# Attention into a SoLU feed-forward on one core: q and k requested a quad ahead, the w_out product later, fewer additions, and a new order for the first quad

## The chip, the cores and the metric

The kernel runs on one core of a Trainium2 chip. The metric is device time in microseconds. Before the change three runs took 1051.24 to 1053.21 us, with a median of 1052.91.

## The reference

Attention with normalised q and k over 8 batches of 12 heads, 448 tokens, 64 wide, and behind it a feed-forward with a SoLU and a layer norm on the 3584 x 768 result. All in float32, while the three feed-forward weights arrive as float64.

```
q_n = q / sqrt(mean(q*q) + 1e-6) * g_q          # k likewise with g_k
attn = softmax(q_n @ k_n.T / 8)                 # per head, 448 x 448
x = (attn @ v), heads side by side              # 3584 x 768
h = x @ w_in                                    # 3584 x 1024
solu = h * softmax(h)
ln = (solu - mean) / sqrt(var + 1e-6) * g_ln
out = ln @ w_out                                # 3584 x 768
```

## The kernel before

Two heads of a batch form a pair (48 pairs), two pairs a quad (24 quads, `m`); within a quad the pairs are called a = 2m and b = 2m + 1. A quad is worked through in one hand-written order, line 930 on, in which each engine takes its instructions strictly as they are written:

- `load` (L543) asks for q and k of a pair: eight slices of 56 KB, each made of runs of 32 floats, on SyncE's queue. `load_v` (L558, L559) asks for v of the next quad, `load_w` (L458) for one chunk of a weight.
- `squares` (ScalarE, L564), `row_sums` (VectorE, L569), `swap_sums` and `fold_sums` (GpSimd, L582, L586) give the sums of squares; `rsqrt_seed` (ScalarE, L593 to L595) and `rsqrt_step` (GpSimd, L600 to L603) the reciprocal root; `normalise` (GpSimd, L608) the normalised q and k, through one buffer; `qk_transpose` (VectorE, L618) turns them, and `gain` (ScalarE, L622) scales q. Only then can `scores` of that pair start.
- `scores` (TensorE, L636) puts 128 keys against 448 queries for two heads, three times per pair; `scores_last` (L648) does the last 64 keys of both pairs at once. Each is followed by an exponential on ScalarE (L629) into a tile E. Two PSUM tiles serve the scores in turn.
- `values` and `values_last` (TensorE, L686, L675) multiply with v. `sums` (TensorE, L711) forms the softmax sums by a product with ones; `add` (L662, L665) adds E tiles up beforehand, so that fewer products are needed. `inverse` and `divide` (VectorE, L719 to L736, GpSimd, L725) finish x.

While the first quads run, the weights are converted from float64 by bits, chunk by chunk: `low_bits` (ScalarE, L473, L474), `high_bits` (VectorE, L477, L478), `join` (VectorE, L482), and for w_out a `product` with g_ln (ScalarE, L487). The twelve chunks of w_in go with pairs 0 to 11 (`W_IN = 12`), the sixteen of w_out, one or two per pair, with pairs 12 to 21 (`W_OUT = 22`). `begin(n)` starts the chunks of a pair, `step(n)` takes them one of the four steps on, `end(n)` takes them on and then asks for as many new chunks; three raw buffers hold what has arrived.

From quad 6 on, two pieces of feed-forward run in each quad (`ff`: the hidden product L754 in two halves; the maximum L764, exponential L767 and the rest of SoLU follow on VectorE and ScalarE), from quad 11 on up to eight, with the output product (L809) among them. In quads 6 to 9 one half hidden product stands behind `scores_last` and one behind `sums`; quad 10 has the latter alone.

In `add`, pairs before 12 add E0 and E1 on VectorE and leave the rest to two more terms of `sums`; pairs from 12 on add E0 and E1 on GpSimd and two more tiles on VectorE, and `sums` has one term.

Of the kernel before, what the change touches and what calls it, by code (L numbers as in the profile page):

```python
# [14 lines left out]
OP = AluOpType  # L15
# [351 lines left out]
def fast_path(  # L367
# [286 lines left out]

    def add(n, kc):
        d = st[n]
        if kc == 1:
            d["es"] = work.tile([P, 2, S], FP32, tag="es", name="es")  # L660
            e = nc.vector if n < W_IN else nc.gpsimd
            e.tensor_tensor(d["es"], d["E", 0], d["E", 1], OP.add)  # L662
        elif n >= W_IN:
            pp, x = (slice(0, P), d["E", kc]) if kc < NJ else (slice(n % 2 * D, n % 2 * D + D), quads[n // 2]["E", NJ])
            nc.vector.tensor_tensor(d["es"][pp], d["es"][pp], x[pp], OP.add)  # L665

    def values_last(m):

# [22 lines left out]
    def sums(m):  # L691

        d = quads[m]
        early = 2 * m < W_IN
        if early:
            sm = ps_h.tile([P, DFF], FP32, tag="h", name="sm")[:, 0:S]
        else:
            sm = ps_t.tile([P, S], FP32, tag="t", name="sm")
        d["sm"] = sm
        terms = [lambda i: (ones[:, 0], st[2 * m + i]["es"])]  # L700
        if early:
# [146 lines left out]
    def load_next():  # L848
        if len(raws) < len(wq):
            raws.append(load_w(wq[len(raws)]))  # L850
# [13 lines left out]
    def step(n):  # L864
        for c in sets[n]:
            c.pop(0)()

    def end(n):

        step(n)  # L870
        for _ in sets[n]:
            load_next()
        step(n)


    events = []
# [21 lines left out]
    def prepare(n):  # L898
        squares(n)
        row_sums(n)  # L900
        swap_sums(n)
        fold_sums(n)
# [2 lines left out]
    load(1)  # L905
    load_gains()
    setup()
    for _ in range(2):
        load_next()
    load(2)  # L910
    load_next()
    load(3)
    load_v(0)
    with tc.manual_schedule():
        prepare(0)
        squares(1)
        rsqrt_seed(0)
        rsqrt_step(0)
        normalise(0)
        row_sums(1)  # L920
        swap_sums(1)
        fold_sums(1)
        gains()
        qk_transpose(0)
        gain(0)
        rsqrt_seed(1)
        rsqrt_step(1)
        normalise(1)
        at = 0
        for m in range(NQ):  # L930
            a, b = 2 * m, 2 * m + 1
            due = []

            while at < len(events) and len(due) < (8 if a >= W_OUT else 2) and events[at][0] <= a:
                due.append(events[at][1])
                at += 1

            def ff(k):
                for f in due[len(due) * k // 4 : len(due) * (k + 1) // 4]:
                    unit(f)  # L940

            more = m + 1 < NQ
            ring = "o"
            unit(lambda: scores(a, 0))
            if m == 0:
                qk_transpose(1)
            else:
                step(a)
            unit(lambda: scores(a, 1))
            gain(b)  # L950
            if m == 0:
                begin(0)
                prepare(2)
            if a >= W_IN:
                add(a, 1)
            ff(0)
            unit(lambda: scores(a, 2))
            unit(lambda: scores_last(m))
            if a < W_IN:
                add(a, 1)  # L960
            if m == 0:
                begin(1)
                prepare(3)
            else:
                end(a)
                if a >= W_IN:
                    begin(b)
            if a >= W_IN:
                add(a, 2)
            ff(1)  # L970
            unit(lambda: scores(b, 0))
            unit(lambda: scores(b, 1))
            if a >= W_IN:
                add(b, 1)
                add(a, 3)
            elif m == 0:
                step(0)
                end(0)
            ff(2)
            unit(lambda: scores(b, 2))  # L980
            if a < W_IN:
                add(b, 1)
            else:
                add(b, 3)
                add(b, 2)
# [7 lines left out]
            def outputs():  # L993
                values_last(m)
                values(a)
# [8 lines left out]
            if more:  # L1004
                qk_transpose(a + 2)
                begin(a + 2)
                normalise(b + 2)
            if m + 2 < NQ:
                swap_sums(a + 4)
                fold_sums(a + 4)  # L1010
            unit(lambda: values(b))
            if m + 2 < NQ:
                load(b + 4)
                squares(b + 4)
                row_sums(b + 4)
            if more:
                gain(a + 2)
                if b + 2 < W_IN:
                    begin(b + 2)
                qk_transpose(b + 2)  # L1020
            if m + 2 < NQ:
# [5 lines left out]
            if more:  # L1027
# [25 lines left out]
def kernel(  # L1053
# [30 lines left out]

    def bound_scores():

        nc.vector.tensor_tensor(gg[:, 0], gg[:, 0], gg[:, 1], OP.mult)
        nc.vector.tensor_reduce(gmax, gg[:, 0], AX, OP.max, apply_absolute_value=True)
        nc.vector.tensor_scalar(large, gmax[0:1], 80.0 / float(D) ** 0.5, None, OP.is_gt)
        nc.vector.tensor_scalar(within, gmax, 80.0 / float(D) ** 0.5, float(D) ** -0.5, OP.is_le, OP.mult)  # L1090
# [36 lines left out]
```

## Time and profile before

| what | value |
|---|---|
| time, median of 3 runs | 1052.91 us |
| profiled execution | 1053.97 us, span 1052.2 us |
| TensorE busy, mean granted clock | 965.3 us (92%), 0.966 |
| VectorE, ScalarE, GpSimd busy | 536.9, 362.4, 318.4 us |
| DMA | 70.09 MB, mean 67 GB/s |

The program is one stream of quads. Early in the span TensorE has gaps, and its records are longer where the granted clock is low; from about 300 us on it is full. A matmul of this kernel shows as two records, so the four matmuls of one `sums` term are eight records.

### The profile page before, as it was taken

What the parts mean: (1) busy time and instruction counts of PE and PEld (TensorE: products, weight loads), DVE (VectorE), ACT (ScalarE), POOL (GpSimd) and SP (SyncE); (2) the same over time, 40 slices, a digit from 0 to 9 for tenths busy, and PEclk for the clock granted to TensorE, in tenths of its full rate; (3) what the DMA queues carried; (4) which work ended last, traced back from release to release, by engine and by line L of the source; (5) the groups of instructions that cost most, each with busy time, mean ns of one, the idle gap of its engine ahead of it and who ended that gap; (6) DMA issues with size and microseconds to landing.
All of it is one profiled execution on the core that took longest, in us unless ns stands there. A gap on an engine that the chain in (4) does not pass through costs nothing.

```text
span 1052.2 us, 10821 instructions
## 1 busy us (share of the span) xinstructions
PE 965.3 (92%) x3619; PEld 428.6 (41%) x3619; DVE 536.9 (51%) x771; ACT 362.4 (34%) x621; POOL 318.4 (30%) x642
## 2 busy tenths in 40 slices
PE   3797887788699999999999999999999999999997
PEld 1232222233134444444444444444444443455554
DVE  3576767667764353534344454434453643555431
ACT  4566754445532232232233232322323323111110
POOL 2455463455344141413141322324141403100000
PEclk9799998898699999999999999999999999999999
DMA  7555544243321121203030302121120001434410
GB/s 150 130 127 115 121 83 97 66 98 77 71 54 44 40 53 30 49 20 67 16 68 16 67 25 45 37 46 43 40 59 24 18 16 33 155 114 123 132 61 34
DMA packets 235961, 70.09 MB, mean 67 GB/s; under 512 B 225136, under 2 KB 225144, under 8 KB 235896
## 3 DMA queue, kind: packets, MB, share of 16 engines
q1 hardware_dynamic: 228152, 57.84, 25.3%
q10 hardware_dynamic: 7744, 11.47, 2.9%
q8 instruction: 30, 0.49, 0.2%
q14 instruction: 35, 0.29, 0.1%
HBM read 58.27 MB, written 11.01 MB: 66 GB/s over the span
## 4 chain that ended last, share of the span: by engine, by line
PE 74%; DVE 6%; ACT 5%; SPq 5%; POOL 4%; DMA 3%; issue 2%; ACTq 0%; POOLq 0%; DVEq 0%
PE po L809 27%; PE h L754 25%; PE s L636 10%; PE o L686 6%; SPq L543 4%; PE s L648 2%; PE pu L798 2%; ACT E L629 2%; DMA v<-in_v_dram 2%; POOL qkn L608 1%; PE sm L711 1%; PE o L675 1%; ACT sq L564 1%; POOL es L662 1%; DVE qkT L618 1%
## 5 line engine op out<-in xcount | busy, mean ns | idle before, releaser
L809 PE MATMUL po<-w_out,uT 128*128 128x384 f32 x896 | 298.6, 489 | 6.7 <-DVE r L719 3.4
L754 PE MATMUL h<-w_in,xT 128*128 128x512 f32 x672 | 302.2, 599 | 0.0
L809 PEld LDWEIGHTS po<-w_out,uT 128*128 128x128 f32 x896 | 167.9, 190 | 137.6 <-issue 16.7
L636 PE MATMUL s<-qkT 64*128 64x448 f32 x576 | 155.2, 646 | 60.3 <-ACT qkT L622 36.4
L754 PEld LDWEIGHTS h<-w_in,xT 128*128 128x128 f32 x672 | 124.9, 191 | 160.6 <-issue 152.3
L629 ACT ACTIVATE E<-s 128x896 f32<-128x896 f32 x168 | 149.6, 915 | 93.8 <-PE s L636 87.7
L665 DVE TENSOR_TENSOR es<-es,E 128x896 f32<-128x896 f32 (+1 forms) x72 | 78.4, 1089 | 96.0 <-ACT E L629 65.3
L662 POOL TENSOR_TENSOR es<-E 128x896 f32<-128x896 f32 x36 | 76.3, 2118 | 158.4 <-ACT E L629 158.3
L782 POOL TENSOR_TENSOR he<-he,mhalf 128x1 f32<-128x1 f32 x28 | 17.5, 624 | 329.9 <-DVE he L781 329.9
L686 PE MATMUL o<-E,v 128*64 128x448 f32 x576 | 114.0, 545 | 0.0
L636 PEld LDWEIGHTS s<-qkT 64*128 64x128 f32 x576 | 52.0, 205 | 150.8 <-ACT E L629 49.8
L810 ACT COPY y<-po 128x384 f32<-128x384 f32 x56 | 26.8, 479 | 219.6 <-PE po L809 219.6
L800 DVE COPY uT<-pu 128x512 f32<-128x512 f32 x28 | 19.3, 688 | 160.1 <-PE pu L798 92.2
L767 ACT ACTIVATE u<-h,hmax 128x1024 f32<-128x1024 f32 x28 | 31.2, 1114 | 157.0 <-DVE hmax L764 157.0
L569 DVE TENSOR_REDUCE part<-sq 128x28 f32<-128x896 f32 x48 | 51.6, 1074 | 65.6 <-ACT sq L564 65.6
L608 POOL TENSOR_TENSOR qkn<-qk,ny 128x896 f32<-128x896 f32 x47 | 79.7, 1696 | 15.1 <-DMA qk<-in_k_dram 4.0
L764 DVE TENSOR_REDUCE hmax<-h 128x1 f32<-128x1024 f32 x28 | 34.0, 1215 | 82.1 <-PE h L754 82.1
L618 DVE STREAM_TRANSPOSE qkT<-qkn 128x896 f32<-128x896 f32 x48 | 53.1, 1106 | 34.6 <-POOL qkn L608 34.6
L686 PEld LDWEIGHTS o<-E,v 128*64 128x64 f32 x576 | 39.3, 138 | 74.4 <-issue 72.7
L564 ACT ACTIVATE sq<-qk 128x896 f32<-128x896 f32 x48 | 45.5, 949 | 67.7 <-DMA v<-in_v_dram 31.4
L582 POOL COPY ss<-part 32x28 f32<-32x28 f32 x188 | 40.1, 213 | 45.7 <-DVE part L569 26.7
L600 POOL TENSOR_TENSOR nx<-nx,ny 128x28 f32<-128x28 f32 x47 | 24.5, 521 | 89.1 <-ACT ny L595 89.1
(83 smaller groups left out, 705.7 us busy)
## 6 DMA issues: line engine op xcount, KB each, us to landing
qk<-in_q_dram SPq DMA_DIRECT2D x192, 56.0 KB, 2.6
out_dram<-y ACTq DMA_DIRECT2D x28, 384.0 KB, 2.3
qk<-in_k_dram SPq DMA_DIRECT2D x184, 56.0 KB, 2.2
v<-in_v_dram SPq DMA_DIRECT2D x96, 96.0 KB, 2.3
raw<-in_moe_w_in_dram SPq DMA_DIRECT2D x12, 512.0 KB, 4.3
raw<-in_moe_w_out_dram SPq DMA_DIRECT2D x16, 384.0 KB, 3.3
again<-in_moe_w_in_dram SPq DMA_DIRECT2D x13, 448.0 KB, 4.1
again<-in_moe_w_out_dram SPq DMA_DIRECT2D x13, 448.0 KB, 3.4
```

Of the source, the lines that this page charges most:

```text
L543: (nc.scalar if n < 2 and s else nc.sync).dma_start(d["qk"][g * 32 : g * 32 + 32, s], src[b, h0 + g // 2].rearrange("(b t) (x d) -> x t b ...
L564: nc.scalar.activation(d["sq"], d["qk"].rearrange("p s b d -> p (s b) d"), AF.Square)
L569: nc.vector.tensor_reduce(d["part"], d["sq"], AX, OP.add)
L608: first(n).tensor_tensor(d["qkn"], d["qk"].rearrange("p s b d -> p (s b) d"), d["y"].rearrange("p b -> p b ()").to_broadcast([P, 2 * NB, 32]),
L618: nc.vector.transpose(d["qkT"].rearrange("p s t -> p (s t)"), d["qkn"].rearrange("p b d -> p (b d)"))
L629: nc.scalar.activation(d["E", kc], s[:, :, 0:S], AF.Exp)
L636: nc.tensor.matmul(s[:, h, 0:S], d["qkT"][hh, 1, kc * P : (kc + 1) * P], d["qkT"][hh, 0, :], start=True, stop=True)
L662: e.tensor_tensor(d["es"], d["E", 0], d["E", 1], OP.add)
L665: nc.vector.tensor_tensor(d["es"][pp], d["es"][pp], x[pp], OP.add)
L686: nc.tensor.matmul(d["o"][h * D : (h + 1) * D, :], d["v"][:, h, kc], d["E", kc][:, h], start=False, stop=(kc == NJ - 1),)
L754: nc.tensor.matmul(d["h"][:, hs], xTs[m][:, c, i * P : (i + 1) * P], w_in[:, c, hs], start=(c == 0), stop=(c == KD - 1))
L809: nc.tensor.matmul(po, d["uT"][:, c], w_out[:, c, hs], start=(c == 0), stop=(c == KF - 1))
```

## The change

Loads: q and k of pairs a+4 and b+4 are requested together behind the second scores of pair a, no longer each just ahead of its squares. Before the loop the order is chunk, pair 2, pair 3, chunk, v, chunk.

`add`: pairs 12 to 21 now also add E0 and E1 on VectorE and leave the rest to `sums`, whose two more terms last until pair 21; the sums of quads 6 to 10 still use the same PSUM tile as before. From pair 22 on nothing is different.

Weights: the last step of a chunk, the product of w_out, leaves `end` and comes behind the second scores of pair b for pair a, and behind the values of pair b for pair b; the `begin` that follows moves with it.

First quad: pair 0's and pair 1's preparation are interleaved otherwise, the preparation of pairs 2 and 3 moves behind the last scores of pair a and the second of pair b, and the conversions of chunks 0 and 1 move behind the exponentials. Three small instructions on the gains go from VectorE to GpSimd.

```diff
-    def add(n, kc):
+    DVE, POOL = nc.vector, nc.gpsimd
+
+    def add(n, kc, engine):
         d = st[n]
+        busy = n < W_OUT
         if kc == 1:
-            d["es"] = work.tile([P, 2, S], FP32, tag="es", name="es")
-            e = nc.vector if n < W_IN else nc.gpsimd
-            e.tensor_tensor(d["es"], d["E", 0], d["E", 1], OP.add)
-        elif n >= W_IN:
+            if engine is (DVE if busy else POOL):
+                d["es"] = work.tile([P, 2, S], FP32, tag="es", name="es")
+                engine.tensor_tensor(d["es"], d["E", 0], d["E", 1], OP.add)
+        elif not busy:
...
     def sums(m):
...
-        if early:
+        if 2 * m < W_OUT:
             terms = [
...
     def end(n):
         step(n)
         for _ in sets[n]:
             load_next()
-        step(n)
...
     with tc.manual_schedule():
-        prepare(0)
+        squares(0)
+        row_sums(0)
+        swap_sums(0)
+        fold_sums(0)
         squares(1)
+        row_sums(1)
         rsqrt_seed(0)
         rsqrt_step(0)
+        gains()
         normalise(0)
-        row_sums(1)
...
             gain(b)
-            if m == 0:
-                begin(0)
-                prepare(2)
-            if a >= W_IN:
-                add(a, 1)
+            if next2:
+                load(a + 4)
+                load(b + 4)
+            add(a, 1, POOL)
             ff(0)
             unit(lambda: scores(a, 2))
             unit(lambda: scores_last(m))
...
             unit(lambda: scores(b, 1))
-            if a >= W_IN:
-                add(b, 1)
-                add(a, 3)
-            elif m == 0:
-                step(0)
-                end(0)
+            if m:
+                step(a)
+                if a >= W_IN:
+                    begin(b)
+            else:
+                prepare(3)
...
             unit(outputs)
-            if m + 2 < NQ:
-                load(a + 4)
+            if next2:
                 squares(a + 4)
                 row_sums(a + 4)
             end(b)
-            if more:
+            if next1:
                 qk_transpose(a + 2)
-                begin(a + 2)
+                if a < W_IN:
+                    begin(a + 2)
                 normalise(b + 2)
...
+            step(b)
+            if next1:
+                if a >= W_IN:
+                    begin(a + 2)
                 if b + 2 < W_IN:
                     begin(b + 2)
```

SyncE's queue before, from the last v of quad 0's end to the first of quad 1's; buffer numbers tell pairs apart: qk_502 and qk_537 are pairs 6 and 7, raw is a chunk.

```order
L558 DMA v_402<-in_v_dram 128x3x64 x2
L559 DMA vl_397<-in_v_dram 64x2x64
L458 DMA raw_449<-in_moe_w_in_dram 128x1024
L543 DMA qk_502<-in_q_dram 32x14x32 x4
L543 DMA qk_502<-in_k_dram 32x14x32 x4
L458 DMA raw_516<-in_moe_w_in_dram 128x1024
L543 DMA qk_537<-in_q_dram 32x14x32 x4
L543 DMA qk_537<-in_k_dram 32x14x32 x4
L558 DMA v_576<-in_v_dram 128x3x64 x2
```

The same place after the change; qk_434 and qk_443 are pairs 6 and 7.

```order
L558 DMA v_402<-in_v_dram 128x3x64 x2
L559 DMA vl_397<-in_v_dram 64x2x64
L543 DMA qk_434<-in_q_dram 32x14x32 x4
L543 DMA qk_434<-in_k_dram 32x14x32 x4
L543 DMA qk_443<-in_q_dram 32x14x32 x4
L543 DMA qk_443<-in_k_dram 32x14x32 x4
L458 DMA raw_467<-in_moe_w_in_dram 128x1024
L458 DMA raw_525<-in_moe_w_in_dram 128x1024
L558 DMA v_576<-in_v_dram 128x3x64 x2
```

The sixteen slices moved ahead of both chunks, and v stays last.

ScalarE before, in quad 6, from the gain of pair b to the last exponential; L629 are the exponentials, L487 the product of pair a's w_out chunk, L473 and L474 the low bits of pair b's two.

```order
L622 ACTIVATE qkT<-qkT,gcol 128x448
L629 ACTIVATE E<-s 128x896 x2
L487 ACTIVATE w_out<-tmp,gcol 128x384
L473 ACTIVATE tmp<-raw,seven 128x384
L474 ACTIVATE tmp<-tmp 128x384
L473 ACTIVATE tmp<-raw,seven 128x384
L474 ACTIVATE tmp<-tmp 128x384
L629 ACTIVATE E<-s 128x896 x3
```

The same after the change.

```order
L622 ACTIVATE qkT<-qkT,gcol 128x448
L629 ACTIVATE E<-s 128x896 x4
L487 ACTIVATE w_out<-tmp,gcol 128x384
L473 ACTIVATE tmp<-raw,seven 128x384
L474 ACTIVATE tmp<-tmp 128x384
L473 ACTIVATE tmp<-raw,seven 128x384
L474 ACTIVATE tmp<-tmp 128x384
L629 ACTIVATE E<-s 128x896
```

Product and low bits moved behind two more exponentials: those of pair b's first two scores.

## Rows read from the trace of the kernel before

**Rows 1.** Windows: stretch, its length, busy us of PE, PEld, DVE, ACT, POOL, clock, DMA
```profile
15.40:43.48 28.08, 19.16 (x89) 5.69 (x89) 11.35 (x14) 16.20 (x29) 14.28 (x30) 0.86 0.63 136
43.48:139.16 95.68, 80.98 (x440) 26.37 (x440) 69.33 (x91) 63.97 (x105) 48.31 (x120) 0.92 0.58 124
139.16:298.70 159.54, 129.37 (x469) 44.22 (x469) 113.94 (x157) 79.69 (x139) 75.75 (x134) 0.86 0.38 79
298.70:1052.20 753.50, 735.58 (x2623) 352.12 (x2622) 335.61 (x493) 198.07 (x342) 177.94 (x342) 1.00 0.20 52
```

**Rows 2.** Waits, 43.48 to 139.17: who for whom, us in total, times, longest
```profile
DVE part L569 <- ACT sq L564: 24.8, 11, 4.0
...
PE s L636 <- ACT qkT L622: 18.6, 6, 4.8
```

**Rows 3.** Timeline of quad 2: start, length, engine and line, [idle before, releaser]
```profile
62.86 4.10 PE L636 MATMUL s<-qkT 64*128 64x448 f32 x12 [2.25 <-ACT qkT L622]
...
76.45 2.26 SPq L543 DMA_DIRECT2D qk<-in_k_dram  x4
...
77.26 1.71 PE L711 MATMUL sm<-E,ones 128*32 128x448 f32 x16
77.35 1.10 DVE L618 STREAM_TRANSPOSE qkT<-qkn 128x896 f32<-128x896 f32 x1
...
78.78 0.93 PE L711 MATMUL sm<-es,ones 128*32 128x448 f32 x8
...
80.84 0.95 ACT L564 ACTIVATE sq<-qk 128x896 f32<-128x896 f32 x1 [4.84 <-DMA v<-in_v_dram]
...
81.70 0.65 ACT L622 ACTIVATE qkT<-qkT,gcol 128x448 f32<-128x448 f32 x1
...
82.41 4.17 PE L636 MATMUL s<-qkT 64*128 64x448 f32 x12 [2.69 <-ACT qkT L622]
```

**Rows 4.** Waits, 139.17 to 298.7
```profile
ACT w_out L487 <- DVE tmp L482: 42.5, 10, 6.1
...
DVE es L665 <- POOL es L662: 22.4, 5, 5.7
...
PE s L636 <- ACT qkT L622: 14.6, 5, 4.9
```

**Rows 5.** Timeline, quads 7, 8 and 10
```profile
185.80 2.08 POOL L662 TENSOR_TENSOR es<-E 128x896 f32<-128x896 f32 x1 [6.45 <-ACT E L629]
...
202.67 1.86 PE L636 MATMUL s<-qkT 64*128 64x448 f32 x4 [4.87 <-ACT qkT L622]
...
208.27 1.86 PE L636 MATMUL s<-qkT 64*128 64x448 f32 x4 [1.62 <-ACT E L629]
...
211.76 5.94 PE L754 MATMUL h<-w_in,xT 128*128 128x512 f32 x12
...
284.21 1.87 PE L636 MATMUL s<-qkT 64*128 64x448 f32 x4 [6.09 <-ACT E L629]
```

**Rows 6.** Timeline of quad 0
```profile
20.80 0.74 ACT L473 ACTIVATE tmp<-raw,seven 128x512 f32<-128x512 uint32 x1
...
21.57 0.63 ACT L474 ACTIVATE tmp<-tmp 128x512 int32<-128x512 f32 x1
...
29.59 0.92 ACT L629 ACTIVATE E<-s 128x896 f32<-128x896 f32 x1 [1.16 <-PE s L636]
...
37.72 0.94 PE L711 MATMUL sm<-es,ones 128*32 128x448 f32 x8
...
41.91 0.95 ACT L564 ACTIVATE sq<-qk 128x896 f32<-128x896 f32 x1 [4.33 <-DMA v<-in_v_dram]
```

**Rows 7.** Timeline, SyncE's queue behind a chunk
```profile
36.16 3.71 SPq L543 DMA_DIRECT2D qk<-in_k_dram  x4
```

**Rows 8.** The page's groups (line, count, busy, mean ns) and DMA issues (KB, us to landing)
```profile
L665 DVE TENSOR_TENSOR es<-es,E 128x896 f32<-128x896 f32 (+1 forms) x72 | 78.4, 1089 | 96.0 <-ACT E L629 65.3
...
raw<-in_moe_w_in_dram SPq DMA_DIRECT2D x12, 512.0 KB, 4.3
```

More of the change, by code (lines that the diff above doesn't have):

```diff
@@ L651, in scores_last @@
         exponentials(quads[m], NJ, s)
-    def add(n, kc):
+    DVE, POOL = nc.vector, nc.gpsimd
+    def add(n, kc, engine):
         d = st[n]
+        busy = n < W_OUT
         if kc == 1:
-            d["es"] = work.tile([P, 2, S], FP32, tag="es", name="es")
-            e = nc.vector if n < W_IN else nc.gpsimd
-            e.tensor_tensor(d["es"], d["E", 0], d["E", 1], OP.add)
-        elif n >= W_IN:
+            if engine is (DVE if busy else POOL):
+                d["es"] = work.tile([P, 2, S], FP32, tag="es", name="es")
+                engine.tensor_tensor(d["es"], d["E", 0], d["E", 1], OP.add)
+        elif not busy:
             pp, x = (slice(0, P), d["E", kc]) if kc < NJ else (slice(n % 2 * D, n % 2 * D + D), quads[n // 2]["E", NJ])
-            nc.vector.tensor_tensor(d["es"][pp], d["es"][pp], x[pp], OP.add)
+            engine.tensor_tensor(d["es"][pp], d["es"][pp], x[pp], OP.add)
     def values_last(m):
@@ L693, in sums @@
         d = quads[m]
-        early = 2 * m < W_IN
-        if early:
+        if 2 * m < W_IN:
             sm = ps_h.tile([P, DFF], FP32, tag="h", name="sm")[:, 0:S]
@@ L700, in sums @@
         terms = [lambda i: (ones[:, 0], st[2 * m + i]["es"])]
-        if early:
+        if 2 * m < W_OUT:
             terms = [
@@ L907, in fast_path @@
     setup()
-    for _ in range(2):
-        load_next()
+    load_next()
     load(2)
+    load(3)
     load_next()
-    load(3)
     load_v(0)
+    load_next()
     with tc.manual_schedule():
-        prepare(0)
+        squares(0)
+        row_sums(0)
+        swap_sums(0)
+        fold_sums(0)
         squares(1)
+        row_sums(1)
         rsqrt_seed(0)
         rsqrt_step(0)
+        gains()
         normalise(0)
-        row_sums(1)
         swap_sums(1)
         fold_sums(1)
-        gains()
-        qk_transpose(0)
-        gain(0)
         rsqrt_seed(1)
@@ L928, in fast_path @@
         normalise(1)
+        qk_transpose(0)
+        gain(0)
         at = 0
@@ L940, in ff, with outputs @@
                     unit(f)
-            more = m + 1 < NQ
+            def outputs():
+                values_last(m)
+                values(a)
+            next1 = m + 1 < NQ
+            next2 = m + 2 < NQ
             ring = "o"
             unit(lambda: scores(a, 0))
-            if m == 0:
+            if m:
+                step(a)
+            else:
                 qk_transpose(1)
-            else:
-                step(a)
             unit(lambda: scores(a, 1))
             gain(b)
-            if m == 0:
-                begin(0)
-                prepare(2)
-            if a >= W_IN:
-                add(a, 1)
+            if next2:
+                load(a + 4)
+                load(b + 4)
+            add(a, 1, POOL)
             ff(0)
@@ L958, in fast_path @@
             unit(lambda: scores_last(m))
[L959 to L963, printed above, removed]
-            else:
-                end(a)
-                if a >= W_IN:
-                    begin(b)
-            if a >= W_IN:
-                add(a, 2)
+            add(a, 1, DVE)
+            if m:
+                end(a)
+            else:
+                prepare(2)
+            add(a, 2, DVE)
             ff(1)
@@ L972, in fast_path @@
             unit(lambda: scores(b, 1))
-            if a >= W_IN:
-                add(b, 1)
-                add(a, 3)
-            elif m == 0:
-                step(0)
-                end(0)
+            if m:
+                step(a)
+                if a >= W_IN:
+                    begin(b)
+            else:
+                prepare(3)
+            add(b, 1, POOL)
+            add(a, 3, DVE)
             ff(2)
             unit(lambda: scores(b, 2))
[L981 to L985, printed above, removed]
-            if more:
+            add(b, 1, DVE)
+            add(b, 3, DVE)
+            add(b, 2, DVE)
+            if next1:
                 rsqrt_seed(a + 2)
@@ L991, in fast_path @@
                 rsqrt_step(b + 2)
-            def outputs():
-                values_last(m)
-                values(a)
+            if m == 0:
+                begin(0)
+                step(0)
+                end(0)
+                begin(1)
             step(b)
             unit(outputs)
-            if m + 2 < NQ:
-                load(a + 4)
+            if next2:
                 squares(a + 4)
@@ L1003, in fast_path @@
             end(b)
-            if more:
+            if next1:
                 qk_transpose(a + 2)
-                begin(a + 2)
+                if a < W_IN:
+                    begin(a + 2)
                 normalise(b + 2)
-            if m + 2 < NQ:
+            if next2:
                 swap_sums(a + 4)
@@ L1011, in fast_path @@
             unit(lambda: values(b))
-            if m + 2 < NQ:
-                load(b + 4)
+            if next2:
                 squares(b + 4)
                 row_sums(b + 4)
-            if more:
+            if next1:
                 gain(a + 2)
+            step(b)
+            if next1:
+                if a >= W_IN:
+                    begin(a + 2)
                 if b + 2 < W_IN:
@@ L1020, in fast_path @@
                 qk_transpose(b + 2)
-            if m + 2 < NQ:
+            if next2:
                 swap_sums(b + 4)
@@ L1026, in fast_path @@
             later(2, lambda m=m: divide(m))
-            if more:
+            if next1:
                 load_v(m + 1)
@@ L1085, in bound_scores @@
     def bound_scores():
-        nc.vector.tensor_tensor(gg[:, 0], gg[:, 0], gg[:, 1], OP.mult)
+        nc.gpsimd.tensor_tensor(gg[:, 0], gg[:, 0], gg[:, 1], OP.mult)
         nc.vector.tensor_reduce(gmax, gg[:, 0], AX, OP.max, apply_absolute_value=True)
-        nc.vector.tensor_scalar(large, gmax[0:1], 80.0 / float(D) ** 0.5, None, OP.is_gt)
-        nc.vector.tensor_scalar(within, gmax, 80.0 / float(D) ** 0.5, float(D) ** -0.5, OP.is_le, OP.mult)
+        nc.gpsimd.tensor_scalar(large, gmax[0:1], 80.0 / float(D) ** 0.5, None, OP.is_gt)
+        nc.gpsimd.tensor_scalar(within, gmax, 80.0 / float(D) ** 0.5, float(D) ** -0.5, OP.is_le, OP.mult)
     fast_path(tc, q, k, v, moe_w_in, moe_w_out, out, grow, within, large, load_gains, bound_scores)
```

## The prediction

> **What bounds the kernel now.** I read the stage windows first, cut where TensorE begins the first scores of quad 0, 1, 6 and 11 [rows 1]. From 298.70 us on TensorE is busy 735.58 of 753.50 us at clock 1.00: that part is TensorE's own work, and nothing in this change takes work from it. Before that, three stretches are not full. Quad 0 takes 28.08 us; quads 1 to 5 take 95.68 us (19.1 each) with TensorE busy 80.98 at a mean granted clock of 0.92; quads 6 to 10 take 159.54 us (31.9 each) with TensorE busy 129.37 at 0.86. So the time of this kernel is the moment at which quad 11 starts, plus a tail that stays. The change lives wholly ahead of that moment.
>
> The waits come next. In quads 1 to 5 TensorE stands 18.6 us, at six starts of a quad, for ScalarE's scaling of the next q (`gain`), and VectorE stands 24.8 us for ScalarE's squares [rows 2]. The timeline of quad 2 shows the place [rows 3]: SyncE issues the k slices of pair b+4 from 76.45 to 78.71; ScalarE's squares begin at 80.84 after 4.84 us idle (the row names the v load, but squares read q and k alone); the gain that follows in ScalarE's queue begins at 81.70; and TensorE, through with its sums at 78.78 + 0.93 = 79.71, starts quad 3 at 82.41 after 2.69 us idle. The transpose that the gain really needs was ready at 77.35 + 1.10 = 78.45. A load that is issued just ahead of its use holds up an unrelated instruction behind it.
>
> In quads 6 to 10 the same wait is there (14.6 us, five starts) beside two others [rows 4]: ScalarE stands 42.5 us, in ten places, for VectorE's join before it can scale a w_out chunk, and VectorE stands 22.4 us for GpSimd's addition.
>
> **The change, part by part.** All sums are against the profiled execution, 1053.97 us (a span of 1052.2 and 1.77 around it), which is 1.06 above the median of the three runs.
>
> *q and k asked for early.* Sixteen issues move from two places late in a quad to one place behind its second scores; the two chunks of a quad and v come behind them in SyncE's queue, as its order shows. The four buffers allow it: the buffer of pair a+4 was last read by pair a's normalise, in the quad before. In [rows 3] the gain could then end at 78.45 + 0.03 + 0.65 = 79.13, which is 0.6 us ahead of TensorE's 79.71. So the 2.69 us go whole, but with only 0.6 to spare; next late is VectorE's transpose behind GpSimd's normalise. Over the stretch: 18.6 us of start waits less 4.8 (the longest, quad 1's own, counted below) is 13.8. With the gaps the clock lost after them goes as well: from 0.92 to about 0.97 on 80.98 us is 4 us (an estimate). Against both stands the thin slack, with VectorE busy 69.33 of 95.68 in strict order. I take 13; the ends are 4 (a new wait takes most of it) and 21 (TensorE full: 95.68 - 80.98 x 0.92).
>
> Newly late: a chunk of w_in is issued behind sixteen slices. Four slices take 2.26 us [rows 3], so sixteen take about 9, and a chunk takes 4.3 us to land [rows 8]: it is there some 14 us into the quad. ScalarE first reads it right behind the gain, 79.13 - 62.86 = 16.3 us in at today's pace and about 14 if the quad shrinks to 16.5. That hides it, with nothing to 2 us over.
>
> *The first quad.* Row sums of pair 1 go ahead of pair 0's reciprocal root, so GpSimd starts earlier on pair 1; I count 1.2 us for that. Two conversions, 0.74 + 0.63 us each on ScalarE, go behind the exponentials instead of among them: 2.8 us [rows 6]. So the last exponential ends near 26.5 and not at 29.59 + 0.92 = 30.5. VectorE's three scalar instructions that go to GpSimd weigh under 0.5 us either way. At the end of the quad squares waited 4.33 us for data (41.91) while TensorE was free from 37.72 + 0.94 = 38.66 on [rows 6]. With the data there, ScalarE has two seeds, three conversions, two squares and the gain behind the last exponential, about 9 us with a wait for the row sums: quad 1 starts near 36, not 43.48. I take 7; the ends are 3.5 (only the front gains) and 10.
>
> *Fewer additions, and the product later, quads 6 to 10.* Per pair VectorE loses two additions and takes over GpSimd's: ten fewer in all at 1.09 us [rows 8], and GpSimd loses ten of 2.08. The GpSimd one at 185.80 stood ahead of the reciprocal root and so of the next quad's normalise [rows 5]. TensorE gets two terms more per quad, sixteen records, 1.71 us by [rows 3], so 8.6 us over five quads, which only earlier starts can pay for. The gains: the start waits, 14.6 less 2.9 for quad 6's own start, which the stretch before has counted, are 11.7. Inside quads 7 to 9, 9.1 us pass today from the first scores (202.67) to the hidden product (211.76) [rows 5]: VectorE reaches the maximum of the hidden row late, ScalarE's exponentials stand behind that, and TensorE waits 1.62 us for them at 208.27. With VectorE idle early I count 6.6, so 2.5 x 3 = 7.5. In quad 10, which has no hidden product in its middle, the scores wait 6.09 us for ScalarE (284.21) [rows 5], which the w_out product held; with the product behind the second exponential about 6 go. That makes 25.2 - 8.6 = 16.6, and a clock of 0.90 in place of 0.86 on 129.37 us gives some 5 more. The product now stands ahead of pair b's third exponential, up to 3.4 us with the low bits behind it, but TensorE has the value products of pair a meanwhile. I take 18; the ends are 4 and 39 (159.54 - 129.37 x 0.86 - 8.6).
>
> A rule of the Trainium skill speaks against the addition that VectorE takes over: the page "GPSIMD Engine Reference", section "Specifications", says that GpSimd shares its SBUF interfaces with VectorE and contends with VectorE instructions that have two SBUF inputs. By it the addition would stretch GpSimd's next work rather than spare it. The trace has no such pair of instructions apart from all else, and the sum stands without the rule.
>
> *After quad 11.* The same work, with requests only earlier: 0, and 3 either way.
>
> Sum: 7 + 13 + 18 = 38; 1053.97 - 38 = 1016 for a profiled execution, 1015 beside the median. The rivals are given beside the median too.
>
> **Rivals.**
> A. The wait changes its name. Normalise and transpose alternate through one buffer, the gain stays late by them, and half of each term is lost: 19 us, 1034. For it: the 0.6 us of slack. Against: VectorE's 24.8 us for the squares go too, so the transposes move forward. That the requests are not early at all, held in the queue by v's wait for the value products, would end here as well.
> B. TensorE becomes nearly full in all three stretches: 8 + 19 + 27 = 54, 999. Against: inside quads 6 to 10 the maximum, the exponentials and the scores still form a chain.
> C. No change: the chunks land late by what the squares gave back, and the 8.6 us of sums eat the rest: about 1052.
> D. Slower: SyncE becomes the bound of quads 1 to 5. Its 24 issues a quad at some 0.5 us are 12 of 19 us, but four slices behind a chunk took 3.71 us [rows 7], 0.93 each. At x us an issue a quad takes 24x + 0.7, as chunks and v stand behind the burst. With 18 + 3.5 gained elsewhere it ends slower from x = 0.96 on; at 1.1 it is 5 x 8.0 - 21.5 = 18.5 up, 1071. Against: only slices directly behind a chunk were that slow, and such places go from two a quad to one.
>
> A page stands behind D: the Trainium skill's "DMA: Bandwidth & Descriptors", section "Specifications", puts line rate at 512 B and more per transfer, and q and k come here in runs of 128 B. By that the burst would be slow by itself; the trace, with four slices in 2.26 us, does not show it.
>
> **Chances.** Forecast (1008 to 1026) 0.62, A 0.20, B 0.10, C 0.04, D 0.04. The range that leaves out 2 in 10 takes the forecast, most of A and part of B: 1003 to 1036. About 0.2% (2 us) is what a measurement of this kernel can tell from no change: faster 0.92, same 0.04, slower 0.04.
>
> **What would show it.** Right: no wait of ScalarE ahead of squares; TensorE's wait for the gain under 5 us in all; quad 1 starting near 36, quad 6 near 119, quad 11 near 261; the sums of quads 6 to 10 with 24 records and no GpSimd addition beside them. Wrong: ScalarE's low bits waiting for a chunk (D), starts waiting for the transpose (A), quad 11 starting after 285, or a tail longer than 756 us.

## The result and the profile after

The change brings the median from 1052.08 us (1050.24 to 1053.21, four runs) to 1006.88 us (1005.37 to 1007.75, four runs): a ratio of 0.957, interval 0.955 to 0.959. The forecast was 1015, with 1008 to 1026 as its own range and 1003 to 1036 as the wide one: the result lies in the wide one alone. The profiled execution took 1006.18 us, with a span of 1004.4 and TensorE at a mean clock of 0.995 (0.966 before).

Windows of the changed kernel, cut at the same instructions as [rows 1] (first scores of quad 0, 1, 6 and 11), with the same columns:

```profile
15.52:37.54 22.02, 16.64 (x88) 5.54 (x89) 12.47 (x14) 15.69 (x26) 10.81 (x23) 0.96 0.80 180
37.54:118.41 80.87, 79.38 (x441) 25.60 (x441) 68.49 (x91) 63.77 (x105) 54.38 (x121) 0.97 0.70 150
118.41:250.28 131.87, 122.20 (x553) 44.05 (x549) 92.62 (x147) 78.83 (x139) 48.26 (x130) 1.00 0.45 96
250.28:1004.40 754.12, 735.59 (x2623) 352.32 (x2622) 333.67 (x493) 197.94 (x342) 178.27 (x342) 1.00 0.20 52
```

Quad 1 starts 5.94 us earlier than before, quads 1 to 5 take 14.81 less, quads 6 to 10 27.67 less, and what follows 0.62 more: 47.8 of span in all. Each stretch splits into time in which TensorE stood (length less busy) and busy time. In quads 1 to 5 the standing fell from 14.70 to 1.49 us and busy time from 80.98 to 79.38. In quads 6 to 10 the standing fell from 30.17 to 9.67, and busy time from 129.37 to 122.20 although the sums have 80 records more: the clock rose from 0.86 to 1.00.

The waits of the changed kernel, first from 37.54 to 118.41 us:

```profile
ACT qkT L622 <- DVE qkT L618: 7.7, 5, 1.7
...
PE s L636 <- ACT qkT L622: 4.5, 1, 4.5
```

and from 118.41 to 250.28:

```profile
PE s L636 <- ACT E L629: 8.0, 9, 1.7
...
ACT w_out L487 <- DVE tmp L482: 2.3, 1, 2.3
```

TensorE's six start waits of [rows 2] have become one, that of quad 1. The 42.5 us in which ScalarE stood for joins [rows 4] are 2.3, and the start waits and VectorE's wait for GpSimd's addition are gone from the second list. What is left to TensorE there are waits for exponentials: nine of the scores, 8.0 us in all, and one of the values, 1.7. The end of quad 2 shows how narrow the first success is (compare [rows 3]):

```profile
68.30 1.10 DVE L618 STREAM_TRANSPOSE qkT<-qkn 128x896 f32<-128x896 f32 x1
...
69.34 0.93 PE L713 MATMUL sm<-es,ones 128*32 128x448 f32 x8
69.44 0.67 ACT L622 ACTIVATE qkT<-qkT,gcol 128x448 f32<-128x448 f32 x1 [1.50 <-DVE qkT L618]
...
70.20 1.77 PE L636 MATMUL s<-qkT 64*128 64x448 f32 x8
```

The gain ends at 70.11, TensorE's sums at 70.27: 0.16 us to spare, and the gain now waits for the transpose, not for squares.

### The profile page after: what moved, and what is told of

It reads as the page before. It is cut to its first block, busy times and chain, and to the rows that moved or that the text cites. A ratio compares the mean times of both kernels' runs of the same rounds, so it can differ in the third digit from the quotient of the medians.

```text
span 1004.4 us, 10943 instructions
## 1 busy us (share of the span) xinstructions
PE 954.0 (95%) x3699; PEld 427.7 (43%) x3699; DVE 513.7 (51%) x758; ACT 361.1 (36%) x621; POOL 296.0 (29%) x635
## 2 busy tenths in 40 slices
DMA packets 235962, 70.11 MB, mean 70 GB/s; under 512 B 225136, under 2 KB 225144, under 8 KB 235896
## 4 chain that ended last, share of the span: by engine, by line
PE 83%; DVE 6%; ACT 4%; POOL 3%; DMA 2%; SPq 1%; issue 1%; ACTq 0%; POOLq 0%; DVEq 0%
PE h L756 29%; PE po L811 28%; PE s L636 9%; PE o L689 8%; PE pu L800 2%; PE sm L713 2%; PE s L648 2%; PE o L678 2%; ACT E L629 1%; POOL qkn L608 1%; DVE qkT L618 1%; SPq L543 1%; POOL ss L582 1%; DMA v<-in_v_dram 1%; DVE w_in L482 1%
## 5 line engine op out<-in xcount | busy, mean ns | idle before, releaser
L629 ACT ACTIVATE E<-s 128x896 f32<-128x896 f32 x168 | 149.4, 915 | 103.7 <-PE s L636 99.8
L636 PE MATMUL s<-qkT 64*128 64x448 f32 x576 | 139.7, 589 | 22.3 <-ACT qkT L622 10.7
L668 DVE TENSOR_TENSOR es<-es,E 128x896 f32<-128x896 f32 (+1 forms) x52 | 56.5, 1087 | 75.1 <-ACT E L629 67.5
L665 POOL TENSOR_TENSOR es<-E 128x896 f32<-128x896 f32 x26 | 55.7, 2144 | 127.0 <-ACT E L629 127.0
L636 PEld LDWEIGHTS s<-qkT 64*128 64x128 f32 x576 | 48.3, 190 | 104.4 <-issue 44.3
L582 POOL COPY ss<-part 32x28 f32<-32x28 f32 x188 | 44.4, 236 | 16.3 <-DVE part L569 7.7
```

Source lines behind the costliest of these rows:

```text
L582: first(n).tensor_copy(d["ss"][g * 32 : g * 32 + 32], d["part"][o * 32 : o * 32 + 32])
L629: nc.scalar.activation(d["E", kc], s[:, :, 0:S], AF.Exp)
L636: nc.tensor.matmul(s[:, h, 0:S], d["qkT"][hh, 1, kc * P : (kc + 1) * P], d["qkT"][hh, 0, :], start=True, stop=True)
L665: engine.tensor_tensor(d["es"], d["E", 0], d["E", 1], OP.add)
L668: engine.tensor_tensor(d["es"][pp], d["es"][pp], x[pp], OP.add)
```

## The experiments

Starts of quads are read as the first scores of each; before and after the change they stand in the windows. The kernel before was run beside every group, with medians of 1053.6 to 1054.7 us. Times are medians, with the lowest and highest in brackets.

The windows of quads 6 to 10 end where quad 11 begins, and quad 11 is not the same in all runs. Its length is 48.79 us in the changed kernel, and from 46.1 to 52.8 in the others. Near its start TensorE's transposes (L800) wait for VectorE, by their rows for the division of quad 10's values (L738):

```profile
253.69 0.66 PE L800 MATMUL pu<-ident,u 128*128 128x128 f32 x4 [1.64 <-DVE xT L738]
255.10 0.66 PE L800 MATMUL pu<-ident,u 128*128 128x128 f32 x4 [0.75 <-DVE xT L738]
```

A run that loses time in quad 10 can be without these waits, and one whose VectorE is late has longer ones. So where it matters quads 6 to 11 are given too: 180.66 us in the changed kernel.

**The early requests alone**, in the kernel before:

```diff
             gain(b)
+            if m + 2 < NQ:
+                load(a + 4)
+                load(b + 4)
...
-                load(a + 4)
                 squares(a + 4)
...
-                load(b + 4)
                 squares(b + 4)
```

> The kernel before, with one thing changed: q and k of pairs a+4 and b+4 are requested behind the second scores of pair a. Theory (the late data of the squares holds the gain, and the gain holds the next quad): quads 1 to 5 fall from 95.7 us to 81 to 83, as in the changed kernel; the end of quad 0 gains about 4; in quads 6 to 10 the start waits fall from 11.7 to about 5, since the product of w_out still stands ahead of the second squares in ScalarE's queue; together about 24 us, 1028. Rival (the new order of VectorE and ScalarE is what closes the gaps, the early request alone moves the wait to the transpose): quads 1 to 5 stay above 90 us, 1045 or more.

1024.03 us (1023.23 to 1025.39), ratio 0.971 [0.969, 0.974]. Quad 1 starts at 36.95, quads 1 to 5 take 80.71, quads 6 to 10 149.73. So the requests alone give all that the first quad and quads 1 to 5 gained, and 9.8 of the 27.7 us behind.

**The changed kernel with the late requests**, the same edit in the other direction:

> The changed kernel, with the requests for q and k put back ahead of their squares. Theory: the start waits of quads 2 to 6 return, 13.8 us and some 3 of clock, and quad 0 loses 0 to 1, so quads 1 to 5 take about 97 us and the whole 1022 to 1026. In quads 6 to 10 little returns, since the gain ends about 5 us ahead of TensorE there (194.20 against 199.05). Rival (the requests carry the gain of quads 6 to 10 too): 1035 or more.

1031.17 us (1029.8 to 1034.22), ratio 0.979 [0.976, 0.982]. Quads 1 to 5 take 93.60 (about 97 expected) and quads 6 to 10 134.00, 2.1 more, as expected. But quad 1 starts at 46.40, 8.9 us later, where 0 to 1 was expected, and the time is above the 1022 to 1026. Of the 8.9, 1.0 is the start of quad 0, which is that much later in this run. Without the requests quad 0 takes 29.88 us in the new order and 28.08 in the old: the new one is worse, with ScalarE waiting twice for data:

```profile
39.70 0.95 ACT L564 ACTIVATE sq<-qk 128x896 f32<-128x896 f32 x1 [5.94 <-DMA qk<-in_k_dram]
...
44.84 0.95 ACT L564 ACTIVATE sq<-qk 128x896 f32<-128x896 f32 x1 [2.89 <-DMA qk<-in_k_dram]
```

**The changed kernel with the first quad as before** (the order ahead of the loop, the preparation of pairs 2 and 3, the first conversions, the instructions on the gains):

```diff
-        squares(0)
-        row_sums(0)
-        swap_sums(0)
-        fold_sums(0)
+        prepare(0)
...
+            if m == 0:
+                begin(0)
+                prepare(2)
             add(a, 1, POOL)
...
```

> The changed kernel with the first quad and the bounds on the scores laid out as before; loads, product and additions stay changed. Theory (the new layout brings nothing by itself; the early loads alone brought quad 1 forward, as the run with the loads alone shows with a start at 36.95 us): quad 1 starts at 36.5 to 38, the rest is unchanged, 1006, give or take 2. Rival (the prediction's own step: the front of the quad gains 3.5 us by the order of row sums and conversions): quad 1 starts at 40 to 41 and the time is about 1010.

1005.55 us (1005.07 to 1007.56), ratio 0.954 [0.952, 0.956]; quad 1 starts at 37.01. The new layout brings nothing: the difference from the changed kernel's time is within the spread of the runs. It does bring TensorE's own work forward, but not the start. In the changed kernel:

```profile
32.13 0.94 PE L713 MATMUL sm<-es,ones 128*32 128x448 f32 x8
...
37.54 3.36 PE L636 MATMUL s<-qkT 64*128 64x448 f32 x8 [4.47 <-ACT qkT L622]
```

and in this one:

```profile
35.67 0.94 PE L713 MATMUL sm<-es,ones 128*32 128x448 f32 x8
37.01 1.77 PE L636 MATMUL s<-qkT 64*128 64x448 f32 x8 [0.41 <-ACT qkT L622]
```

The 3.5 us are there, as the wait of 4.47 for the gain. What the gain waits for stands in VectorE's queue of the changed kernel:

```profile
34.09 1.08 DVE L569 TENSOR_REDUCE part<-sq 128x28 f32<-128x896 f32 x1
...
35.08 0.68 DVE L482 TENSOR_TENSOR w_in<-tmp 128x512 uint32<-128x512 uint32 x1
...
35.68 1.10 DVE L618 STREAM_TRANSPOSE qkT<-qkn 128x896 f32<-128x896 f32 x1
...
36.82 0.67 ACT L622 ACTIVATE qkT<-qkT,gcol 128x448 f32<-128x448 f32 x1 [0.67 <-DVE qkT L618]
```

GpSimd had finished the normalised q and k by 32.51. The transpose comes 3.2 us later, behind row sums and a join, and these need ScalarE's squares and low bits first.

**The first quad rearranged further**, so that this gain comes earlier:

```diff
...
+                if m == 0:
+                    swap_sums(3)
+                    fold_sums(3)
+                    qk_transpose(2)
                 rsqrt_seed(b + 2)
                 rsqrt_step(b + 2)
             if m == 0:
+                gain(2)
                 begin(0)
...
```

> The changed kernel with one more rearrangement of the first quad alone: transposes and scaling of pair 2 go ahead of the first two conversions, and the fold of pair 3's row sums goes behind the normalising of pair 2. Theory (the start of quad 1 at 37.54 us is set by the row sums of pair 3 in GpSimd's queue and by the conversions ahead of the scaling): quad 1 starts at 33 to 34.5, the time is 1002 to 1004. Rival (TensorE's own work of quad 0, 16.65 us busy from 15.5 on, and the conversions that now come late set it): quad 1 starts at 36 or later, or what is won is lost in quad 1 again, 1005.5 to 1008.

1010.08 us (1008.38 to 1010.62), ratio 0.958 [0.956, 0.960]. Quad 1 does start at 33.74, and quad 2 at 57.10 in place of 54.44. The conversions, late now, stand ahead of quad 1's first exponentials:

```profile
33.74 1.77 PE L636 MATMUL s<-qkT 64*128 64x448 f32 x8 [0.43 <-ACT qkT L622]
42.09 1.87 PE L636 MATMUL s<-qkT 64*128 64x448 f32 x4 [6.57 <-ACT E L629]
```

The rival held in kind, with a larger loss than it named. ScalarE's work up to quad 2 is the same in either order, so the earlier start moved the wait behind it; behind that wait four records of scores took 1.87 us. By the start of quad 2 the changed kernel's profile is 2.7 us ahead of this one's; the medians are 3.2 apart.

**The changed kernel with the old additions and sums of pairs 12 to 21**:

```diff
-        busy = n < W_OUT
+        busy = n < W_IN
...
-        if 2 * m < W_OUT:
+        if 2 * m < W_IN:
```

> The changed kernel, with the additions of pairs 12 to 21 as before: GpSimd adds E0 and E1, VectorE two more, and the sums of quads 6 to 10 have one term. Theory 1 (with 5 us between gain and TensorE the additions fit, and TensorE saves 8.6 us): faster than the changed kernel by 4 to 8 us, 999 to 1003, quads 6 to 10 in 124 to 128 us instead of 131.9. Theory 2, the one of the prediction (the GpSimd addition ahead of the reciprocal root holds up the next quad): start waits of 1 to 3 us return in quads 6 to 10 with half clock behind them, and the time is 1007 to 1015.

1016.13 us (1014.63 to 1017.37), ratio 0.964 [0.961, 0.967]; quads 6 to 10 take 142.37, 10.5 more (10.4 through quad 11). The time is just above the range of theory 2. The records that the sums save do not come back as time. Two more runs split this cost.

**GpSimd makes the first addition, the rest stays in the sums**:

```diff
-            if engine is (DVE if busy else POOL):
+            if engine is (DVE if n < W_IN else POOL):
```

> The changed kernel with one thing of the additions put back: in quads 6 to 10 GpSimd makes the first addition of a pair (2.08 us) again, in place of VectorE; the other additions stay in TensorE's sums. Theory (the 10 us that the old additions cost come from GpSimd's addition, behind which VectorE's next work and GpSimd's own seeds wait): quads 6 to 10 take 139 to 142 us in place of 131.9 and the time is 1013 to 1016. Rival (they come from VectorE's twenty additions behind it): quads 6 to 10 stay at 131 to 134 us, 1005 to 1008.

1009.02 us (1008.19 to 1009.66), ratio 0.956 [0.954, 0.958]; quads 6 to 10 take 137.21, 5.3 more, all of it in quad 10 (29.21 in place of 23.88). VectorE and GpSimd there:

```profile
234.51 0.35 DVE L477 TENSOR_SCALAR tmp<-raw 128x384 uint32<-128x384 uint32 x1
...
234.90 0.56 DVE L478 SCALAR_TENSOR_TENSOR tmp<-raw,tmp 128x384 uint32<-128x384 uint32 x1
235.28 4.29 POOL L665 TENSOR_TENSOR es<-E 128x896 f32<-128x896 f32 x2
235.38 2.24 DVE L477 TENSOR_SCALAR tmp<-raw 128x384 uint32<-128x384 uint32 x1
237.66 2.33 DVE L478 SCALAR_TENSOR_TENSOR tmp<-raw,tmp 128x384 uint32<-128x384 uint32 x1
```

and TensorE behind them:

```profile
245.36 1.76 PE L689 MATMUL o<-E,v 128*64 128x448 f32 x4 [4.29 <-ACT E L629]
```

The same two conversions take 0.35 and 0.56 us by themselves and 2.24 and 2.33 beside GpSimd's addition, 3.66 us more. The join, the product of the chunk and pair b's third exponential stand behind them in turn, and TensorE's values wait 4.29 us where the changed kernel waits 1.66. That is 2.6 of the 5.3 us. The other 2.7 are the clock behind this wait: it is 0.50 from 245.36 to 247.05, and the four records of values take 1.76 us (0.97 in the changed kernel). Quad 11 then takes 46.12 us, without the waits at its start, so that through quad 11 the addition costs 2.7 and not 5.3; the medians are 2.1 apart. Neither range held. In quads 7 to 9, which take 27.35 each as without it, conversions are stretched as well (to 1.86 and 2.24), and it costs nothing.

**All three additions on VectorE, one term in the sums** (the expectation counts four a pair and thirty more in all; there are three, and twenty more than in the changed kernel):

```diff
-        elif not busy:
+        elif n >= W_IN:
...
-        if 2 * m < W_OUT:
+        if 2 * m < W_IN:
```

> The changed kernel with all four additions of a pair on VectorE in quads 6 to 10 and one term in TensorE's sums: GpSimd adds nothing, VectorE has 30 additions more than in the changed kernel, TensorE 16 records fewer a quad (1.7 us). Theory (GpSimd's addition was the cost, VectorE has the room): quads 6 to 10 take 130 to 134 us, 1004 to 1008. Rival (VectorE's queue is the cost, whoever made the first addition): 139 us or more, 1013 or more.

1013.82 us (1012.01 to 1014.33), ratio 0.960 [0.958, 0.962]; quads 6 to 10 take 135.83, 4.0 more, now in quads 7 to 9 (86.65 in place of 82.04). Quad 11 takes 52.77 us, with VectorE late there too, so through quad 11 it is 7.9 more. The time is the rival's, the window neither side's. With 2.7 from GpSimd's addition and 7.9 from VectorE's queue through quad 11 both are costs, VectorE's queue the larger, and together they come to the 10.4 of the old additions. In quads 6 to 10 VectorE comes late to the inverse of the sums and to the hidden maximum, and TensorE's scores wait for each:

```profile
173.95 1.02 PE L636 MATMUL s<-qkT 64*128 64x448 f32 x4 [0.77 <-DVE r L721]
177.44 1.86 PE L636 MATMUL s<-qkT 64*128 64x448 f32 x4 [2.46 <-ACT E L629]
```

**The changed kernel with product and low bits ahead, as before**:

```diff
     def end(n):
         step(n)
         for _ in sets[n]:
             load_next()
+        step(n)
...
+                if a >= W_IN:
+                    begin(b)
...
-            if m:
-                step(a)
-                if a >= W_IN:
-                    begin(b)
```

> The changed kernel, with the product of w_out and the low bits that follow it back ahead of the first exponential of pair b, and the other ones ahead of the second squares. Theory: ScalarE's product waits for VectorE's join until 183.2 in quad 8 and the low bits follow, so the first exponential of pair b starts 2 to 3 us late in each of quads 6 to 9 and about 6 late in quad 10; TensorE waits as long: 12 to 18 us, 1019 to 1025. Rival (it is hidden in the hidden product, as the other chain is): under 3 us, 1007 to 1010.

1014.98 us (1014.07 to 1016.67), ratio 0.963 [0.960, 0.966]; quads 6 to 10 take 144.32, 12.5 more, of which 8.3 are quad 10's, where the scores wait behind the product (the answer to the last of [rows 5]):

```profile
246.64 1.87 PE L636 MATMUL s<-qkT 64*128 64x448 f32 x4 [7.39 <-ACT E L629]
```

More than the rival's 3 us, less than expected in quads 6 to 9 (4.2 in all). Quad 11 gives 2.7 back (46.11), so it is 9.8 through quad 11, and the time is below the 1019 that was expected at least.

**Fewer records in the sums.** In quads 6 to 10 pair a alone is added up on VectorE, so that its groups of the sums have one term and pair b's three:

```diff
-        elif not busy:
+        elif not busy or (n >= W_IN and n % 2 == 0):
...
+                    if alone and i == 0 and x < len(terms) - 1:
+                        continue
...
```

> The changed kernel, in which in quads 6 to 10 pair a alone is added up on VectorE as before (two additions of 1.09 us a quad more, one term of its row sums in place of three: 8 records of TensorE fewer, 0.86 us a quad). Theory A (these two additions stand where VectorE idles, 2.4 us ahead of the next quad's transposes, and cost nothing): quads 6 to 10 take 127.5 to 129 us, the time is about 1002.5. Theory B (any addition put back into VectorE's queue delays what follows, the hidden maximum first): 132 to 138 us, 1006 to 1012.

1008.8 us (1008.18 to 1010.21), ratio 0.957 [0.955, 0.959]; quads 6 to 10 take 131.80. Neither held in these quads: nothing is lost on VectorE, and nothing is won on TensorE. Its chain:

```profile
191.84 2.38 PE sm L716 x15
194.22 5.36 PE h L762 x12
```

The sums take 2.38 us with 16 records (15 of them on the chain) as they took 2.40 with 24 (191.31 to 193.71 in the changed kernel). Rows of the four groups, which fill 32 output partitions each, run side by side, and the group with three terms sets the time. (Quad 11 takes 50.55 us here; the run with the old first quad, which has the changed kernel's code from quad 1 on, took 50.51. So a difference of this size there comes and goes between executions, and the median's 1.9 us over the changed kernel is not shown to be a cost of the additions.)

**Two terms for all**: VectorE adds the third exponential too.

```diff
-        elif not busy:
+        elif not busy or (n >= W_IN and kc == 2):
...
```

> The changed kernel, in which VectorE adds the third exponential of each pair of quads 6 to 10 too, so that the sums have two terms there (16 records of TensorE fewer is 0.86 us less a quad on each of two pairs together, 4.3 us in all). Theory A (VectorE has room ahead of the hidden maximum, which comes 1.67 us late only by TensorE): quads 6 to 10 take 127 to 129 us in place of 131.9, and the time is about 1003. Theory B (VectorE's queue sets the pace of these quads, as the run with the old additions suggests): ten additions of 1.09 us delay the maximum, quads 6 to 10 take 133 to 138 us, and the time is 1008 to 1013.

1010.62 us (1007.64 to 1012.33), ratio 0.959 [0.956, 0.961]; quads 6 to 10 take 131.54. Here the sums do shrink (165.94 to 167.58, 1.64 us), but the scores wait 2.46 us for the exponential in two quads where they waited 1.66, and quad 11 takes 52.79, its scores and transposes waiting for VectorE. Through quad 11 it is 3.7 us more. The time is theory B's: what TensorE saved stands in its next wait.

**The row sums behind the hidden product.** That 1.66 us is the chain of the hidden maximum, its exponential and the scores' exponential, at the start of quads 7 to 10. In quad 8 of the changed kernel:

```profile
171.71 1.77 PE L636 MATMUL s<-qkT 64*128 64x448 f32 x8
175.14 1.02 PE L636 MATMUL s<-qkT 64*128 64x448 f32 x4 [1.66 <-ACT E L629]
...
177.40 2.84 PE L756 MATMUL h<-w_in,xT 128*128 128x512 f32 x6
```

This run puts the sums beside that chain:

```diff
+            if W_IN <= a < W_OUT:
+                ff(3)
+                unit(lambda: (sums(m), inverse(m)))
+                later(0.5, lambda m=m: divide(m))
+            else:
...
```

> The changed kernel with one reordering in quads 6 to 10: the hidden product at the end of a quad goes ahead of the row sums, so that the hidden row's maximum and exponential run beside the sums (2.4 us) and not beside the next quad's first scores. Theory (the 1.66 us that TensorE stands in each of quads 7 to 10 is the chain maximum, exponential of the hidden row, exponential of the scores, and has the sums' 2.4 us to hide behind): that wait goes, quads 7 to 9 take 25.7 us each in place of 27.35, quads 6 to 10 about 125, the time is 998 to 1001. Rival (another chain takes its place: the inverse of the sums now stands between the maximum and the moments on VectorE, and the second scores' buffer is held by the sums until it is done): 0 to 2 us are won, 1004 to 1007.

1001.66 us (1001.55 to 1003.86, five runs), ratio 0.950 [0.948, 0.951], the fastest here: all its runs lie below all of the changed kernel's. Quads 7 to 9 take 25.99 each in place of 27.35, quads 6 to 10 127.56. At the end of quad 8 and the start of quad 9 its TensorE:

```profile
172.76 1.02 PE L636 MATMUL s<-qkT 64*128 64x448 f32 x4 [0.17 <-ACT E L629]
...
188.97 5.42 PE L756 MATMUL h<-w_in,xT 128*128 128x512 f32 x12
194.32 1.71 PE L713 MATMUL sm<-E,ones 128*32 128x448 f32 x16
195.85 0.94 PE L713 MATMUL sm<-es,ones 128*32 128x448 f32 x8
196.72 1.49 PE L636 MATMUL s<-qkT 64*128 64x448 f32 x6
```

The wait went from 1.66 to 0.17, as the theory had it; it overstated the sum (4.3 us won in quads 6 to 10, 6.9 expected), as quads 6 and 10 gain nothing. In quad 10 the wait of the values grew to 2.77.

**The same with two terms:**

> The run with the row sums behind the hidden product, and with VectorE adding the third exponential too in quads 6 to 10, so that the sums have two terms there (16 records in place of 24, 0.86 us less a quad). Theory (with the maximum hidden beside the sums TensorE is the bound of these quads, and what it saves shows): quads 7 to 9 take 25.1 us each in place of 25.98, quads 6 to 10 about 123.5, the time is 997 to 999. Rival (VectorE's queue, ten additions longer, brings the maximum late, or the shorter sums no longer hide it, as with the third addition alone): quads 6 to 10 take 127 us or more, 1001 to 1006.

1006.3 us (1005.85 to 1008.14, five runs), ratio 0.957 [0.955, 0.958]; quads 6 to 10 take 129.16. The rival held, with a time 0.3 us above its range: with the third addition VectorE reaches the inverse later, and the sums hold the PSUM tile that the second scores need:

```profile
172.83 1.02 PE L636 MATMUL s<-qkT 64*128 64x448 f32 x4 [1.16 <-DVE r L720]
```

## Why the prediction was right, and which of its terms were not

**The bound and the mechanism** were right: the time is the start of quad 11 plus a tail that stays (754.12 us, 753.50 before), and the waits that were to go went. Contrary to what was named as a sign, ScalarE's squares still stand, once in each of quads 2 to 10, by 0.9 to 1.4 us: pair b's go into the one buffer from which VectorE still forms pair a's row sums. The time is halfway between the 1015 and rival B's 999, and in quads 6 to 10 it is B's 27 that came.

**Quads 1 to 5:** 14.8 against 13. The standing fell by 13.2 (13.8 reckoned), the clock gave 1.6 (4 reckoned), although it did rise to the 0.97 that was reckoned: busy time scaled by a mean clock, in which the standing is counted too, gave too much here. The slack of the gain, reckoned at 0.6, is 0.16, and next late is what was named: VectorE's transpose. The run with the requests alone shows that they are the whole cause. D fell: four slices take about 2.1 us, and no low bits wait for a chunk.

**The first quad:** 5.9 against 7, with the wrong split. The step that failed is "the front gains", in which an earlier last exponential was passed on to the start of quad 1. The last exponential does end at 26.48, as reckoned, and TensorE's part did move by 3.5 us; but the start is set by the conversions, squares and row sums that stand ahead of the transpose and the gain on ScalarE and VectorE. That the sum came near is luck. The requests alone give 36.95, the old layout with them 37.01, the new one 37.54.

**Quads 6 to 10:** 27.7 against 18; this term is 9.7 of the 9.8 us by which the 1016 for a profiled execution was too high. By its parts: the standing fell by 20.5 us, where 25.2 were reckoned; the sums' extra records were put at 8.6; and with these the busy time should have been 129.37 + 8.6 = 137.97, where 122.20 was measured, so the clock gave 15.8 (an estimate, since it leans on the 8.6), where 5 were reckoned. The prediction took a clock of 0.90 for the stretch after the waits had gone; the profile shows 1.00. The mis-sized term is the clock. In quads 7 to 9 the hidden product followed 5.7 us behind the first scores (6.6 reckoned, 9.1 before).

Of the cover for product and low bits the prediction said that pair a's values stand over pair b's third exponential. That holds in quads 7 to 9; in quad 10 it fails by 1.66 us:

```profile
241.63 0.97 PE L689 MATMUL o<-E,v 128*64 128x448 f32 x4 [1.66 <-ACT E L629]
```

**The additions.** The prediction saw GpSimd's addition as a delay of the next quad's normalise. The runs show two other costs: conversions stretched beside it in quad 10, and VectorE's queue ahead of the inverse and the maximum in quads 7 to 9. The rule of the Trainium skill on shared SBUF interfaces was set aside because the trace was said to have no such pair of instructions apart from all else. It has one, in the kernel before:

```profile
212.63 2.11 POOL L662 TENSOR_TENSOR es<-E 128x896 f32<-128x896 f32 x1
212.72 2.23 DVE L477 TENSOR_SCALAR tmp<-raw 128x384 uint32<-128x384 uint32 x1
```

The conversion ends 0.21 us behind the addition; the one just ahead of it (211.85) took 0.35. The Trainium skill ("GPSIMD Engine Reference", section "Specifications") names VectorE instructions in a two-port mode or with two SBUF inputs. The run with GpSimd's additions agrees for the conversion that reads two tiles, 0.56 to 2.33 us; for the one that reads a single tile, 0.35 to 2.24, no row tells the mode. The rule was an argument for the change.

**The parts do not add up.** Alone, the requests are worth 9.8 us in quads 6 to 10; taken away last, they are worth 2.1, the additions 10.5 and the product 12.5 (the last two 10.4 and 9.8 through quad 11). The late requests cost little because the gain has room with the rest changed: that of quad 9 ends at 194.20, and TensorE comes to it at 199.05. The additions or the product alone, in the kernel before, were not run.

## What to carry to other kernels

Ask for data so early that no instruction waits for it in a queue in which something unrelated stands behind; that was the larger part here, 28 of the 45 us, and one edit. Before bringing a start forward, find what ends last at it: work moved on one engine, the total of another unchanged, comes back as the next wait. To hide a chain through three engines, look for independent work of the bound engine to put beside it, before cutting that work.

## What the runs showed of the hardware beyond that

- GpSimd's addition of two 128x896 tiles stretched VectorE's conversions of 128x384 from 0.35 to 2.24 and from 0.56 to 2.33 us. Which of the two is held goes by which began first. In the kernel before, VectorE's L786 took 2.56 us where it began 0.07 behind GpSimd's addition (374.39) and 0.81 where it began 0.18 ahead of it (350.32); there the addition took 2.57 in place of 2.08.
- Matmuls that write different groups of 32 output partitions overlap: 16 records in uneven groups took 2.38 us, 24 in even ones 2.40, 16 in even ones 1.64. A count of records is no price. The Trainium skill says as much ("TensorEngine Tiling (Array Packing)", section "Tiling Modes": tiles work independently), and the rows agree.
- The clock in quads 6 to 10 was 0.86 before and 1.00 after, over the whole stretch. One wait shows its price: in the run with all additions on VectorE, four records of scores took 1.86 us behind a wait of 2.46, at a granted clock of 0.50, and 1.02 behind one of 0.77, at 1.00. These are the lower of the clock's two levels (1.2 GHz) and the upper (2.4 GHz).
- Nearly the same waits can leave the clock up or down. At the start of quad 11 the transposes waited 1.64 and 0.75 us in the changed kernel, and up to the next scores the clock was 1.00; they waited 1.67 and 0.76 in the run with the old first quad, and it was 0.86, for 1.7 us more.
